# Top-32 attention and a feed-forward block on one core: VectorE turns both heads of 72 units at the end of a step, GpSimd gets the smaller scores as a difference to the larger, and TensorE's filling follows an estimate of VectorE's step

## The chip, the cores and the metric

The kernel runs on one core of one Trainium2 chip. A core has five engines that run side by side, each with its own in-order queue: TensorE (PE; its weight loads are shown as PEld), VectorE (DVE), ScalarE (ACT), GpSimd (POOL), and SyncE (SP), which here only issues DMAs. The metric is the device time of one execution in microseconds, lower is better. A profile is of one execution; "span" is the time from its first to its last instruction.

## The reference

Attention over 8 batches, 8 heads, 576 positions and a head size of 64, in which each row keeps its 32 largest scores; then a normalised feed-forward block of width 512 and 2048. All is float32.

```python
scores = scale * np.matmul(q, k.transpose(0, 1, 3, 2))
kth = np.partition(scores, -top_k, axis=-1)[..., -top_k:-top_k + 1]     # top_k = 32
scores = np.where(scores >= kth, scores, -1e9)
attn = np.exp(scores - np.max(scores, axis=-1, keepdims=True))
attn = attn / (np.sum(attn, axis=-1, keepdims=True) + 1e-09)
x = heads side by side of np.matmul(attn, v)                            # (8, 576, 512)
xn = (x - mean) / np.sqrt(var + 1e-06) * g_ln
out = x + np.maximum(xn @ w_ch1, 0.0) @ w_ch2
```

## The kernel before

**Units and steps.** Two heads are handled together. Their 576 query rows make four units of 128 rows (numbers 0 to 3) and one of 64 rows, the rest unit, which packs both heads into 128 partitions. There are 160 units. They come in groups that are multiplied with the values together: from the third batch on, the first half of a batch has four groups of units 0, 1 and rest, the second half four groups of units 2 and 3. The main loop makes one step per unit, and all engines' work is written out by hand in the order of that loop.

**A unit's way.** Unit n has its scores made by TensorE at step n-1 (`scores`: eight matmul records at line 354 into PSUM, four ScalarE copies at line 335 into the tile `sc`). Also at step n-1 `halve` splits its 576 scores into 288 pairs: VectorE takes the larger of each pair (line 376, tile `hi`), GpSimd the smaller (tile `lo`) with integer arithmetic on the bits, as a + b (line 375) minus the larger (line 377). At step n VectorE looks for the 32 largest: `select` with argument 0 works on `lo` (lines 390 and 385), with 1, 2 and 3 on `hi` (lines 398 and 385). At step n+1 ScalarE makes the mask (`mask`, line 442, tile `e`), at step n+2 the exponential with its row sum (`weigh`, line 452). At step n+2 the weights are also turned, so that keys lie on partitions (tile `pt`), and at the third step after a group's last unit `values` multiplies them with the values (lines 563 and 570).

**Turning.** `turn` gives a list of parts: four TensorE transposes for each head (line 505) with a ScalarE copy out of PSUM (line 517 for head 0, 521 for head 1), and a last one for the columns left over (lines 538 and 539). From batch 2 on, 72 units (`u.moved`: whole units that are not the last of their group) have head 1 turned otherwise, by `move`: VectorE transposes 32x32 blocks (line 482, written into the unit's own `sc`, which is free by then), SP stores the result in DRAM (line 487) and reads it back in another order into `pt` with four DMAs (line 489). `move` stands after `select(u, 0)`, early in the step, and `weigh` takes head 1 first for these units.

**Filling.** The feed-forward work on finished rows is a list of small pieces, `todo`: "hidden" matmuls at line 680 and "project" matmuls at line 697. `fill` is called eight times a step and issues pieces up to a share, `slot(n)`. Until all weights are converted (the first 18 steps) the share is the difference of the two estimates `dve_cost` and `pe_cost`; after that it is an equal amount for each step up to the next delivery of rows (`gives`), with `RESERVE` us of work kept back.

**Other names.** `prepare` makes the exponential's bias (lines 436 and 437), on VectorE for the first 17 units, on GpSimd for the others. `turn_heads` (line 304) transposes K and Q of the next pair of heads on VectorE; behind it SP loads the pair after that, eight DMAs. `stats` (lines 629 to 638) normalises finished rows, `recips` are reciprocals of row sums (line 932). Tiles of one name share a few buffers: `sc` has four, `hi` two, `lo`, `pt` one.

Of the kernel before, what the change touches and what calls it, by code (L numbers as in the profile page):

```python
# [29 lines left out]
def kernel(  # L30
# [332 lines left out]
    def halve(u):  # L363

        nt = len(u.tiles)  # L370
        u.lo = lopool.tile([P, 2, HALF], FP32, tag="lo", name="lo")
        u.hi = hipool.tile([P, 2, HALF + TOP_K // 2], FP32, tag="hi", name="hi")
        a, b = u.sc[:, 0:nt, 0:HALF], u.sc[:, 0:nt, HALF:S]
        lo, hi = u.lo[:, 0:nt], u.hi[:, 0:nt, 0:HALF]
        nc.gpsimd.tensor_tensor(lo.bitcast(I32), a.bitcast(I32), b.bitcast(I32), ALU.add)  # L375
        nc.vector.tensor_tensor(hi, a, b, ALU.max)  # L376
        nc.gpsimd.tensor_tensor(  # L377
            lo.bitcast(I32), lo.bitcast(I32), hi.bitcast(I32), ALU.subtract
        )

    def select_halved(u, i):
        nt = range(len(u.tiles))
# [46 lines left out]
    def prepare(u):  # L429

        nt = len(u.tiles)
        u.bias = small.tile([P, 2], FP32, tag="bias", name="bias")
        b = u.bias[:, 0:nt]

        engine = nc.vector if u.i < CONVERTING else nc.gpsimd
        engine.tensor_tensor(b, u.thr[:, 0:nt, 7], u.top[:, 0:nt, 0], ALU.subtract)  # L436
        engine.tensor_scalar(b, b, scale, 0.0, ALU.mult, ALU.add)  # L437

    def mask(u, t):
        if u.e is None:  # L440
# [25 lines left out]
    def place_of(u):  # L466

        g = u.group  # L470
        if g.pt is None:
            g.pt = ptpool.tile([P, 2 * J + 1, GQ], FP32, tag="pt", name="pt")
            g.ptB = g.pt[:, J : 2 * J].rearrange("p c n -> p (c n)").rearrange(
                "p (i c n) -> p i c n", c=J, n=32
            )
        return sum(P for x in g.qts if x < u.qt)

    def move(u):

        i0 = place_of(u) // 32  # L480
        t = u.sc[:, 1, 0:JP]
        nc.vector.transpose(
            t.rearrange("p (j c n) -> p j c n", j=P // 32, c=J),
            u.e[:, 1, R:S].rearrange("p (c j k) -> p j c k", c=J, k=32),
        )
        hbm = hbmpool.tile([P, JP], FP32, tag="turned", name="turned")
        nc.sync.dma_start(hbm[:], t)
        for j in range(P // 32):
            nc.sync.dma_start(
                u.group.ptB[j * 32 : (j + 1) * 32, i0 : i0 + P // 32].rearrange(  # L490
                    "k i c n -> k i (c n)"
                ),
                hbm[:, j * P : (j + 1) * P].rearrange("(i k) x -> k i x", k=32),
            )

    def turn(u):

        g = u.group
        q0 = place_of(u)
        i0 = q0 // 32  # L500

        def part(t):
            ps = turned()
            for c in range(J):
                nc.tensor.transpose(  # L505
                    ps[:, c * P : (c + 1) * P], u.e[:, t, c * P + t * R : (c + 1) * P + t * R],
                    ident[:],
                )
            if u.rest:
                both = ps[:].rearrange("p (c h n) -> p h c n", h=2, n=R)  # L510
                nc.scalar.copy(g.pt[:, 0:J, q0 : q0 + R], both[:, 0])
                nc.scalar.copy(
                    g.ptB[:, i0 : i0 + R // 32],
                    both[:, 1].rearrange("p c (i n) -> p i c n", n=32),
                )
            elif t == 0:
                nc.scalar.copy(  # L517
                    g.pt[:, 0:J, q0 : q0 + P], ps[:].rearrange("p (c n) -> p c n", n=P)
                )
            else:  # L520
                nc.scalar.copy(
                    g.ptB[:, i0 : i0 + P // 32],
                    ps[:].rearrange("p (c i n) -> p i c n", c=J, n=32),
                )

        def last():
            ps = turned()
            if u.rest:
                nc.tensor.transpose(ps[0:R, 0:P], u.e[:, 0, JP:S], ident[:])
                nc.tensor.transpose(ps[:, P : 2 * P], u.e[:, 0, JP - R : S], ident[:])  # L530
                for h in range(2):
                    nc.scalar.copy(
                        g.pt[h * R : (h + 1) * R, 2 * J, q0 : q0 + R],
                        ps[h * R : (h + 1) * R, h * (P + R) : h * (P + R) + R],
                    )
            else:
                ends = u.e[:].rearrange("p t n -> p (t n)")[:, JP : JP + P]
                nc.tensor.transpose(ps[:, 0:P], ends, ident[:])
                nc.scalar.copy(g.pt[:, 2 * J, q0 : q0 + P], ps[:, 0:P])

        heads = [0] if u.moved else range(len(u.tiles))
        return [lambda t=t: part(t) for t in heads] + [last]

    xs, xps, rs, oTr, dr = {}, {}, {}, {}, {}
# [13 lines left out]
    def values(g):  # L558
        vb = g.job.v
        av = brief("av")  # L560
        for c in range(J):
            for h in range(2):
                nc.tensor.matmul(  # L563
                    av[h * D : (h + 1) * D, 0 : g.nq],
                    vb[:, h * J + c, :],
                    g.ptB[:, 0 : g.nq // 32, c, :] if h else g.pt[:, c, 0 : g.nq],
                    start=(c == 0),
                    stop=False,
                )
        nc.tensor.matmul(  # L570
            av[:, 0 : g.nq], g.job.ends[:], g.pt[:, 2 * J, 0 : g.nq],
            start=False, stop=True,
        )
        g.oT = otpool.tile([P, GQ], FP32, tag="oT", name="oT")
        nc.scalar.copy(g.oT[:, 0 : g.nq], av[:, 0 : g.nq])
# [237 lines left out]
                add_block(step, tiles, dsts)  # L813

    SLOTS = 8
    RESERVE = 4.0
    last_give = max(gives)

    def at(i):
# [5 lines left out]
        last = at(n - 2) if n - 2 < EARLY else at(n - 3) if n - 3 >= EARLY else None  # L825
        return turned, last.group if last and last is last.group.units[-1] else None

    DVE_UNIT, DVE_REST, DVE_HALVED, DVE_MOVE = 10.3, 5.3, 0.9, 0.8


    turns = {}
# [4 lines left out]
    def pe_cost(n):  # L836
        c = 0.0
        if at(n + 1):
            c += 1.25 if at(n + 1).rest else 1.5
        ex, g = after(n)  # L840
        if ex:
            c += 0.67 if ex.rest else 0.55 if ex.moved else 1.0
        if g:
            c += 0.6 + 7.8e-3 * g.nq
        return c

    def dve_cost(n):
        u, ex = at(n), after(n)[0]
        c = 5.0 if u is None else DVE_REST if u.rest else DVE_UNIT
        if u and u.halved:  # L850
            c *= DVE_HALVED
        return c + DVE_MOVE if ex and ex.moved else c

    def give(n):
        early = not all(map(done, ready))
# [8 lines left out]
    def slot(n):  # L864


        if n <= CONVERTING:
            return max(0.0, dve_cost(n) - pe_cost(n)) / SLOTS
        left = sum(t[1] for t in todo)
        if n > last_give:  # L870
            even = left / max(1, END - 1 - n)
        else:
            even = 99.0
            for m in sorted(gives):
                if m > n:
                    even = min(even, (left - RESERVE) / (m - n))
                    left += sum(b.cost() for b in gives[m])
        return max(0.0, even) / SLOTS

    recips, rows_of = {}, {}  # L880

# [18 lines left out]
    for n in range(END):  # L900
# [12 lines left out]
        quick = ex.group if last and ex.group.quick else None  # L913

        moved = ex is not None and ex.moved
        order = (1, 0) if moved else (0, 1)
        sent, stores[:] = stores[:], []

        if ex and not early:
            weigh(ex, order[0])  # L920
        if nxt:
            scores(nxt)
        if g:
            values(g)
        if u:
            select(u, 0)
        if moved:
            move(ex)
        for store in sent:
            store()  # L930
        for den in recips.pop(n, []):
            nc.vector.reciprocal(den, den)
        if n == gives_first:
            for blk, i in rows_of.pop(n):
                blk.stats(i)
# [7 lines left out]
            weights(n, 0)  # L943
        fill()
        if ex and len(ex.tiles) > 1 and not early:
            weigh(ex, order[1])
        fill()
        if parts and not moved:
            parts[0]()
# [3 lines left out]
            select(u, 1)  # L953
        if nxt and nxt.halved:
            halve(nxt)
        if n in turns:
            turn_heads(turns[n])
            later = fresh.index(turns[n]) + 1
            if later < len(fresh):
                load(fresh[later], nc.sync, nc.sync)  # L960
        for blk, i in rows_of.pop(n, []):
            blk.stats(i)
        if not quick:
            weights(n, 1)
        fill()
        if mk and not early:
            mask(mk, int(mk.moved))
        if g:
            place(g)
        if late:  # L970
            place_rest(late.job.b, late.job.hp)
        fill(1 if g or late else 0)
        fill()
        if moved:
            parts[0]()
        elif len(parts) > 2:
            parts[1]()
        if u:
            select(u, 2)
        for blk in gives.get(n - 2, []):  # L980
            blk.inverse()
        if last and ex.group.sums is not None:
# [7 lines left out]
        if parts:  # L990
            parts[-1]()
        if mk and len(mk.tiles) > 1 and not early:
            mask(mk, 1 - int(mk.moved))
        fill()
        for x in (u if n < EARLY else None, mk if n > EARLY else None):
            if x and x is units[x.job.last]:
# [9 lines left out]
        if u:  # L1006
            select(u, 3)
            if u.i < CONVERTING:
                prepare(u)
        for x in (g, quick):  # L1010
            if x and x.job.hp == NHP - 1:
                for qt in x.qts:
# [43 lines left out]
```

## Time and profile before

The three runs took 1665.36, 1665.81 and 1666.85 us. The profiled execution has a span of 1666.8 us.

| stretch (us) | what runs | TensorE busy | VectorE busy | ScalarE busy | GpSimd busy |
|---|---|---|---|---|---|
| 0 to 130 | loads, first units, weights converted | 64.4 | 111.8 | 87.5 | 76.2 |
| 130 to 400 | all units turned by TensorE | 252.4 | 262.1 | 203.4 | 146.6 |
| 400 to 1500 | from 428.6 on with `move` | 1096.0 | 1053.1 | 735.9 | 419.1 |
| 1500 to 1667 | last units, then feed-forward alone | 161.3 | 37.6 | 50.4 | 22.1 |

Busy time counts an instruction from its start to its end on its engine. TensorE's matmuls overlap each other and their ends are modelled, so its busy time says that it had no gap, not that it ran at its best. A group line of the profile reads: source line, engine and operation; output tile <- input tile with partitions x elements; count; total busy us and mean ns of one; and how long the engine sat idle just before these instructions, with what ended the idle time.

### The profile page before, as it was taken

What the parts mean: (1) busy time and instruction counts of PE and PEld (TensorE: products, weight loads), DVE (VectorE), ACT (ScalarE), POOL (GpSimd) and SP (SyncE); (2) the same over time, 40 slices, a digit from 0 to 9 for tenths busy, and PEclk for the clock granted to TensorE, in tenths of its full rate; (3) what the DMA queues carried; (4) which work ended last, traced back from release to release, by engine and by line L of the source; (5) the groups of instructions that cost most, each with busy time, mean ns of one, the idle gap of its engine ahead of it and who ended that gap; (6) DMA issues with size and microseconds to landing.
All of it is one profiled execution on the core that took longest, in us unless ns stands there. A gap on an engine that the chain in (4) does not pass through costs nothing.

```text
span 1666.8 us, 25284 instructions
## 1 busy us (share of the span) xinstructions
PE 1574.1 (94%) x7113; PEld 955.1 (57%) x7113; DVE 1464.5 (88%) x4476; ACT 1077.2 (65%) x2759; POOL 664.0 (40%) x879
## 2 busy tenths in 40 slices
PE   3568989989999999999999999999999999999998
PEld 1346556566555575755547575745547575755564
DVE  5998999999999999999999999899998999998000
ACT  5677967767666776767666675767666676665310
POOL 5567854343433434343343434343243433333010
PEclk9758999999999999999999999999999999999999
DMA  7423333001331133213231233112331132111000
GB/s 176 100 64 108 89 58 59 22 14 27 76 81 51 53 76 81 65 54 69 59 86 51 55 73 83 52 54 70 65 89 44 53 81 74 52 46 47 26 13 13
DMA packets 301203, 104.58 MB, mean 63 GB/s; under 512 B 246276, under 2 KB 283144, under 8 KB 301064
## 3 DMA queue, kind: packets, MB, share of 16 engines
q1 hardware_dynamic: 296328, 102.39, 24.4%
q10 hardware_dynamic: 4736, 0.59, 0.3%
q8 instruction: 57, 0.93, 0.2%
q14 instruction: 82, 0.67, 0.1%
HBM read 74.58 MB, written 28.31 MB: 62 GB/s over the span
## 4 chain that ended last, share of the span: by engine, by line
PE 71%; DVE 21%; issue 4%; ACT 2%; POOL 1%; DMA 1%; ACTq 0%; POOLq 0%; DVEq 0%; SPq 0%
PE hps L680 25%; PE ops L697 24%; PE scps L354 8%; PE av L563 6%; DVE m L398 5%; DVE hi L385 4%; PE tp L505 4%; DVE hi L390 2%; DVE m L416 2%; PE av L570 2%; DVE w L423 2%; DVE lo L385 1%; DVE hi L376 1%; DVE size L188 1%; PE tp L667 1%
## 5 line engine op out<-in xcount | busy, mean ns | idle before, releaser
L680 PE MATMUL hps<-xT,w 128*128 128x256 f32 (+1 forms) x2048 | 550.0, 411 | 2.7 <-ACT xT L672 2.3
L697 PE MATMUL ops<-w,h 128*128 128x512 f32 x1152 | 546.1, 599 | 0.0
L398 DVE MAX8 m<-hi 128x8 f32<-128x304 f32 x1088 | 460.7, 458 | 2.3
L680 PEld LDWEIGHTS hps<-xT,w 128*128 128x128 f32 x2048 | 372.1, 191 | 108.5 <-issue 17.3
L385 DVE MATCH_REPLACE8 hi<-m,hi 128x304 f32<-128x304 f32 x816 | 368.0, 456 | 0.0
L375 POOL TENSOR_TENSOR lo<-sc 128x576 int32<-128x576 int32 (+1 forms) x152 | 197.7, 1301 | 316.3 <-ACT sc L335 156.9
L697 PEld LDWEIGHTS ops<-w,h 128*128 128x128 f32 x1152 | 200.2, 191 | 169.9 <-issue 164.6
L377 POOL TENSOR_TENSOR lo<-lo,hi 128x576 int32<-128x576 int32 (+1 forms) x152 | 196.8, 1295 | 141.9 <-DVE hi L376 139.7
L354 PE MATMUL scps<-kT,qT 64*128 64x288 f32 (+3 forms) x1344 | 217.4, 433 | 32.4 <-DVE qT L304 20.9
L335 ACT COPY sc<-scps 128x288 f32<-128x288 f32 x576 | 199.2, 409 | 62.3 <-PE scps L354 51.0
L442 ACT ACTIVATE e<-sc,m 128x576 f32<-128x576 f32 x288 | 224.3, 779 | 9.7 <-DVE m L398 6.2
L452 ACT ACTIVATE e<-e,bias 128x576 f32<-128x576 f32 x288 | 224.6, 780 | 2.9 <-DVE bias L437 2.5
L390 DVE MAX8 hi<-lo 128x8 f32<-128x288 f32 x544 | 221.8, 443 | 2.6 <-POOL lo L377 1.5
L354 PEld LDWEIGHTS scps<-kT,qT 64*128 64x128 f32 (+1 forms) x1344 | 122.4, 181 | 146.6 <-issue 56.2
L505 PEld LDWEIGHTS tp<-ident,e 128*128 128x128 f32 x864 | 110.9, 147 | 115.9 <-ACT e L452 51.7
L505 PE MATMUL tp<-ident,e 128*128 128x128 f32 x864 | 138.1, 285 | 38.2 <-ACT e L452 37.9
L692 ACT ACTIVATE h<-hps 128x256 f32<-128x256 f32 (+1 forms) x256 | 105.9, 414 | 96.5 <-PE hps L680 93.8
L436 POOL TENSOR_TENSOR bias<-m,m 128x2 f32<-128x2 f32 (+1 forms) x143 | 27.8, 195 | 303.6 <-DVE m L398 303.6
L563 PE MATMUL av<-pt,vb 128*64 128x256 f32 (+2 forms) x1088 | 146.7, 413 | 0.0
L376 DVE TENSOR_TENSOR hi<-sc 128x576 f32<-128x576 f32 (+1 forms) x152 | 138.8, 913 | 5.5 <-ACT sc L335 5.5
L385 DVE MATCH_REPLACE8 lo<-hi,lo 128x288 f32<-128x288 f32 x272 | 118.2, 440 | 0.0
L517 ACT COPY pt<-tp 128x512 f32<-128x512 f32 x128 | 74.6, 583 | 62.1 <-PE tp L505 60.5
(79 smaller groups left out, 1295.0 us busy)
## 6 DMA issues: line engine op xcount, KB each, us to landing
turned<-sc SPq DMA_DIRECT2D x72, 256.0 KB, 2.0
pt<-turned SPq DMA_DIRECT2D x288, 64.0 KB, 2.0
vb<-in_v_dram SPq DMA_DIRECT2D x136, 128.0 KB, 2.5
raw<-in_moe_w_ch_dram SPq DMA_DIRECT2D x32, 512.0 KB, 4.0
kin<-in_k_dram SPq DMA_DIRECT2D x128, 72.0 KB, 2.5
qin<-in_q_dram SPq DMA_DIRECT2D x120, 72.0 KB, 2.5
out_dram<-o SPq DMA_DIRECT2D x32, 256.0 KB, 2.2
ends<-in_v_dram SPq DMA_DIRECT2D x136, 16.0 KB, 2.2
```

Source lines behind the costliest of these rows:

```text
L335: nc.scalar.copy(u.sc[:, t, s * HALF : (s + 1) * HALF], made[s][t][:, 0:HALF])
L354: nc.tensor.matmul(ps[i * R : i * R + ql, o : o + width], qT[r, q0 : q0 + ql], kT[r, k0 : k0 + width], start=True, stop=True,)
L375: nc.gpsimd.tensor_tensor(lo.bitcast(I32), a.bitcast(I32), b.bitcast(I32), ALU.add)
L385: nc.vector.match_replace(x[:, t], m[:, t, :], x[:, t], LOWEST)
L390: nc.vector.max(u.hi[:, t, o : o + 8], u.lo[:, t])
L398: nc.vector.max(m[:, t, :], u.hi[:, t])
L442: nc.scalar.activation(u.e[:, t], u.sc[:, t], AF.Prelu, bias=u.thr[:, t, 7:8], scale=-1.0, alpha=SLOPE)
L452: nc.scalar.activation(u.e[:, t], u.e[:, t], AF.Exp, bias=u.bias[:, t : t + 1], scale=-scale / SLOPE, accum_out=g.den[:, col : col + 1],)
L505: nc.tensor.transpose(ps[:, c * P : (c + 1) * P], u.e[:, t, c * P + t * R : (c + 1) * P + t * R], ident[:],)
L563: nc.tensor.matmul(av[h * D : (h + 1) * D, 0 : g.nq], vb[:, h * J + c, :], g.ptB[:, 0 : g.nq // 32, c, :] if h else g.pt[:, c, 0 : g.nq], ...
L680: nc.tensor.matmul(ps["h"][:, 0:N], w1[:, c, f * P : (f + 1) * P], xT[0][:, c, 0:N], start=(c == 0), stop=(c == NC - 1),)
L697: nc.tensor.matmul(ps[i][:], hT[f][:, i * P : (i + 1) * P], w2[:, f, :], start=(f == 0), stop=(f == NF - 1),)
```

## The change

- `halve`: VectorE's maximum comes first. GpSimd then makes a minus the larger, and adds b. Both GpSimd operations now come behind the maximum; before, the first needed only the scores.
- `prepare` for the first 17 units: one fused VectorE instruction per head in place of two instructions for both.
- `move`: both heads of the 72 units are turned by VectorE (two transposes, one store of 512 KB, eight reads), at the end of the step, after `select(u, 3)`. TensorE's four transposes and ScalarE's copy (line 517) for head 0 go; `pt` holds both heads in the same layout of blocks. `weigh` and `mask` take head 0 first for all units.
- Reciprocals move behind `halve`, `stats` behind `select(u, 2)`.
- `slot`: after the first 18 steps the share makes `pe_cost` plus filling a constant multiple of an estimate of VectorE's step, smoothed over three steps (`pace`). The estimates' constants change, `RESERVE` goes from 4 to 7.

```diff
-        nc.gpsimd.tensor_tensor(lo.bitcast(I32), a.bitcast(I32), b.bitcast(I32), ALU.add)
         nc.vector.tensor_tensor(hi, a, b, ALU.max)
         nc.gpsimd.tensor_tensor(
-            lo.bitcast(I32), lo.bitcast(I32), hi.bitcast(I32), ALU.subtract
+            lo.bitcast(I32), a.bitcast(I32), hi.bitcast(I32), ALU.subtract
         )
+        nc.gpsimd.tensor_tensor(lo.bitcast(I32), lo.bitcast(I32), b.bitcast(I32), ALU.add)
...
-        engine = nc.vector if u.i < CONVERTING else nc.gpsimd
-        engine.tensor_tensor(b, u.thr[:, 0:nt, 7], u.top[:, 0:nt, 0], ALU.subtract)
-        engine.tensor_scalar(b, b, scale, 0.0, ALU.mult, ALU.add)
+        if u.i < CONVERTING:
+            for t in range(nt):
+                nc.vector.tensor_scalar(
+                    b[:, t : t + 1], u.thr[:, t, 7:8], u.top[:, t, 0:1], scale,
+                    ALU.subtract, ALU.mult,
+                )
+            return
+        nc.gpsimd.tensor_tensor(b, u.thr[:, 0:nt, 7], u.top[:, 0:nt, 0], ALU.subtract)
+        nc.gpsimd.tensor_scalar(b, b, scale, 0.0, ALU.mult, ALU.add)
...
     def move(u):
-        i0 = place_of(u) // 32
-        t = u.sc[:, 1, 0:JP]
-        nc.vector.transpose(...)
-        hbm = hbmpool.tile([P, JP], FP32, tag="turned", name="turned")
-        nc.sync.dma_start(hbm[:], t)
-        for j in range(P // 32):
-            nc.sync.dma_start(u.group.ptB[j * 32 : (j + 1) * 32, ...], hbm[:, j * P : (j + 1) * P]...)
+        i0 = place_of(u)
+        ni = P // 32
+        for t in range(2):
+            nc.vector.transpose(
+                u.sc[:, t, 0:JP].rearrange("p (j c n) -> p j c n", j=ni, c=J),
+                u.e[:, t, t * R : t * R + JP].rearrange("p (c j k) -> p j c k", c=J, k=32),
+            )
+        hbm = hbmpool.tile([P, 2, JP], FP32, tag="turned", name="turned")
+        nc.sync.dma_start(hbm[:], u.sc[:, :, 0:JP])
+        for j in range(ni):
+            for t in range(2):
+                nc.sync.dma_start(u.group.blocks[j * 32 : (j + 1) * 32, t, i0 : i0 + ni]..., hbm[:, t, ...]...)
...
-        heads = [0] if u.moved else range(len(u.tiles))
+        heads = () if u.moved else range(len(u.tiles))
...
-    DVE_UNIT, DVE_REST, DVE_HALVED, DVE_MOVE = 10.3, 5.3, 0.9, 0.8
+    DVE_UNIT, DVE_REST, DVE_HALVED, DVE_MOVE, DVE_TURN = 9.7, 5.0, 0.89, 1.4, 1.45
...
+    def pace(n):
+        return (dve_cost(n - 1) + 2 * dve_cost(n) + dve_cost(n + 1)) / 4
...
-            for m in sorted(gives):
-                if m > n:
-                    even = min(even, (left - RESERVE) / (m - n))
-                    left += sum(b.cost() for b in gives[m])
-        return max(0.0, even) / SLOTS
+        for k in range(n, last_give):
+            pe += pe_cost(k)
+            dve += pace(k)
+            if k + 1 in gives:
+                ratio = min(ratio, (left - RESERVE + pe) / dve)
+                left += sum(b.cost() for b in gives[k + 1])
+        return max(0.0, ratio * pace(n) - pe_cost(n)) / SLOTS
...
-        if moved:
-            move(ex)
         for store in sent:
             store()
-        for den in recips.pop(n, []):
-            nc.vector.reciprocal(den, den)
...
         if nxt and nxt.halved:
             halve(nxt)
+        for den in recips.pop(n, []):
+            nc.vector.reciprocal(den, den)
...
         if u:
             select(u, 2)
+        for blk, i in rows_of.pop(n, []):
+            blk.stats(i)
...
             select(u, 3)
             if u.i < CONVERTING:
                 prepare(u)
+        if moved:
+            move(ex)
```

## The prediction

> **What bounds the kernel now.** I read the share of busy time first, then the slices, then busy time by stretch, then VectorE's groups and waits.
>
> ```profile
> PE 1574.1 (94%) x7113; PEld 955.1 (57%) x7113; DVE 1464.5 (88%) x4476; ACT 1077.2 (65%) x2759; POOL 664.0 (40%) x879
> PE   3568989989999999999999999999999999999998
> DVE  5998999999999999999999999899998999998000
> ```
>
> Two engines are near full from the fourth slice on, and for the last three slices TensorE works alone. So there are three stages: a start that VectorE leads (to about 409), a long middle, and a TensorE tail. The stretch from the start of VectorE's step 40 (408.7) to that of step 158 (1517.4) is the middle; the second line below is the tail, from TensorE's step 157 on (columns: stretch, length, then busy time of PE, PEld, DVE, ACT, POOL, with counts, then clock, DMA share, GB/s).
>
> ```profile
> 408.70:1517.40 1108.70, 1104.13 (x5023) 661.41 (x5022) 1061.99 (x3319) 741.33 (x1927) 423.81 (x602) 1.00 0.25 65
> 1504.30:1666.80 162.50, 156.95 (x546) 90.64 (x545) 33.37 (x109) 48.14 (x116) 19.70 (x29) 1.00 0.08 24
> ```
>
> In the middle TensorE has no gap to speak of (4.6 of 1108.7 us), VectorE has 46.7. Who is behind?
>
> ```profile
> L482 DVE STREAM_TRANSPOSE sc<-e 128x512 f32<-128x512 f32 x72 | 50.3, 698 | 59.7 <-ACT e L452 59.4
> L376 DVE TENSOR_TENSOR hi<-sc 128x576 f32<-128x576 f32 x120 | 124.6, 1038 | 5.5 <-ACT sc L335 5.5
> L390 DVE MAX8 hi<-lo 128x8 f32<-128x288 f32 x544 | 221.8, 443 | 2.6 <-POOL lo L377 1.5
> 893.38 0.71 DVE L482 STREAM_TRANSPOSE sc<-e 128x512 f32<-128x512 f32 x1 [3.07 <-ACT e L452]
> ```
>
> VectorE waits almost only at the transpose in `move`, for ScalarE's exponential, 2 to 3 us at a time (fourth line, from the timeline). ScalarE is late because TensorE is: the wait comes where three equal portions of filling meet a short rest step. In a triple of steps (units 0, 1, rest, here steps 86 to 88) TensorE's score matmuls start 8.8, 8.0 and 11.0 us apart, 27.8 us; VectorE's own work is 11.0 + 8.3 + 6.2 = 25.5. In a pair (steps 98 and 99) both need 19.3. So TensorE leads by little: adding the gaps over 0.15 us up to 1517.4, VectorE lost 39.7 us and worked 1069.0.
>
> **What the skill says.** "SBUF — State Buffer", section "Who interferes with whom": VectorE with two SBUF inputs and GpSimd reading SBUF hold one shared port as an exclusive lock, and the later one blocks. The trace agrees: line 376's shortest run is 0.74 us, its mean 1.04, its longest 1.95, and the long ones lie beside line 375 on GpSimd; transposes and MAX8, with one input, take the same beside GpSimd (0.457 against 0.459 for MAX8). "VectorE: DVE Perf Modes", section "The three transpose paths": VectorE turns 32x32 blocks only, which is why DRAM has to reorder them; here 0.70 us for four blocks' worth of a head. "DMA: Bandwidth & Descriptors", section on the anatomy of one DMA: about 2 us are fixed, mostly the receipt. Here both DMAs of `move` have a median of 2.0 us to landing, whether 256 KB or 64 KB.
>
> **The change part by part**, against the profiled span of 1666.8, which is 1.0 above the median of the runs.
>
> *Maximum before GpSimd.* In the middle, the 118 runs of line 376 lie 30.2 us in sum above the unhindered 0.745 (whole) and 0.445 (rest); nothing of GpSimd's pair can stand beside them any more. Bounds: 30 gone, or 20 if other GpSimd work (output additions, 1.29 us) gets in the way. I take 30. The price: `lo` is ready later by GpSimd's first operation, 1.43 us. After the maximum GpSimd needs 2.9. In a step of unit 1 or 3 the maximum would start at 3.9 and end at 4.7, `lo` is there at 7.6, and the next step begins at 8.3 to 8.6. A rest step, without the transposes ahead, has 2.4 + 0.75 + 2.9 = 6.1 of 6.85. It fits, except behind an output addition (36 in all): some 0.1 us each, 4 us.
>
> *Second transpose.* 70 of the 72 lie in the middle; two that follow each other start about 0.62 apart (as a move adds 0.60 to a step): +43.4 us on VectorE. On TensorE 4 transposes at 0.109 start to start go: 70 x 0.436 = 30.5. ScalarE loses 72 copies of 0.58, 42 us, but is 67% busy there: nothing, hidden behind both.
>
> *Later place.* The wait of line 482 for ScalarE goes; it stays where ScalarE is a whole step behind: nothing. In its place two things follow the move. First, the `sc` buffer comes free only when the store has landed. By the program's own order of buffers, the copies of the second unit of each triple (24 of them) use a buffer whose store was issued one step end earlier: 2.0 to 2.7 for the landing, 1.2 to 1.5 for four copies, against a maximum at 3.9: 0 to 0.3 us, 4 us in sum. Elsewhere a full step lies between. Second, `pt`: the store, then eight reads at 0.43 on SP, then 2.0 for landing, 2.2 + 3.5 + 2.0 = 7.7 after the move. SP has also the eight K and Q loads (4.0 to 4.9 us behind `turn_heads`) and four of V (2.2) ahead of one move per group, which can hold the store for 0.7 to 1.9: up to 9.6. `values` needs `pt` one step (8.3 to 8.6) and the scores (0.65) later: TensorE is held at 0 to 0.6 us behind VectorE, and VectorE does not notice before it is about 1.9 behind (3.9 less 2.0 for scores and copies). Nothing, with the end kept for a rival.
>
> *Equal multiple.* By the program's order the filling per triple now follows VectorE (about 3.4, 7.8, 6.9 us where it was 6.0, 6.0, 6.0, the small share in the short step). It is the same work; it takes away the reason for VectorE's waits.
>
> *Middle, summed.* VectorE: 1069.0 - 30.2 + 43.4 = 1082.2. TensorE, from scores to scores (409.2 to 1526.2): 1117.0 - 30.5 = 1086.5. The two are within half a percent. I take the larger plus the 8 us of waits: 1094.5, a gain of 14.2.
>
> *Start.* The biases cost VectorE 17 x (0.697 + 0.191) = 15.1 us, since line 436 has two inputs. 34 fused ones with one input should take about 0.17 to 0.19, as line 437 does beside GpSimd: 6, gain 9; if they block like line 436, 34 x 0.7 = 24, loss 9. The maxima of steps 20 to 39 give 3.7. Against it stands that GpSimd is 71% busy from 130 to 260 and its first operation can't start early any more, and that VectorE already waited 4.5 us for scores at step 10. I take a gain of 7, from -3 to 13.
>
> *Tail.* From the scores of unit 158 on the program has 142.9 us of filling where it had 139.5, and 8 transposes fewer: +2.6.
>
> Sum: 1666.8 - 14.2 - 7 + 2.6 = 1648.2, less 1.0 to the median: **1647**.
>
> **Rivals.**
> *A, TensorE alone decides.* For: no gap in the middle; it can be ahead of VectorE at the start and loses less there. Then no wait is seen and the start gives 13, while VectorE's transposes cost 35 instead of 43: middle 1082, 1666.8 - 27 - 13 + 2 - 1 = 1628. Against: VectorE needs 1082 too.
> *B, GpSimd late.* `lo` misses the step start by 0.1 us in most of 118 steps, 12 us, and the start gives nothing: 1647 + 12 + 5 = 1664, no change. Against: 0.7 to 1 us of room in each step.
> *C, slower: the round trip through DRAM.* The chain move, store, eight reads, `values` decides as soon as it lasts more than some 10.5 us after the step's end (8.6 + 1.9), 0.9 above my upper end. The reads' longest issue was 2.1 us and longest landing 3.8, so it can. Then TensorE and after it VectorE stop in each of 48 groups; at 0.6 us, 29 us: 1676. Against: the medians.
> *D, it does not do what it says:* the estimates mislead the filling, and steps mismatch as before, so that 20 of the 39.7 us of waits stay: 1647 + 12 = 1659.
>
> **Chances.** The forecast (1638 to 1656) 0.48, A 0.18, D 0.12, B 0.10, C 0.12. The range 1628 to 1664 leaves C and the edges out. 0.2% is 3.3 us, about what a measurement of this kernel can tell: faster by more 0.79 (forecast, A, most of D, a little of B), within 0.09, slower 0.12.
>
> **What would show it.** Line 376 at a mean of 0.75 for whole units; the transposes of `move` at 144, with no wait above 1 us for ScalarE; TensorE's line 505 at 576 and ScalarE's copy of line 517 gone for moved units; VectorE's idle time in the middle below 20 us. Wrong if VectorE waits at line 376 for `sc`, at line 390 for `lo`, or TensorE at line 563 for a DMA, each for more than 10 us in sum.

## The result, and the profile after

The changed kernel takes 1683.83 us (1679.77 to 1685.19), the kernel before 1666.15 beside it: a ratio of 1.0102, with a 95% interval of 1.0084 to 1.0120. It is 1% slower, where 1% faster was forecast. The profiled execution has a span of 1682.4 us, 15.6 more than before; all sums below are made against the spans.

Start with the page of the changed kernel: busy time by engine, and the slices of TensorE and VectorE.

```profile
PE 1562.3 (93%) x6825; PEld 939.6 (56%) x6825; DVE 1473.0 (88%) x4547; ACT 1032.2 (61%) x2687; POOL 660.8 (39%) x879
PE   3569899999799999999999999999999999999998
DVE  6998999999799999999989999899999999996100
```

TensorE has 288 matmul records less, as it should with 72 x 4 transposes gone, and VectorE is busier by 8.5 us. Neither explains a longer span. Both engines now have a 7 in the eleventh slice (421 to 463), in the middle, where both had 9 before. The chain of waits, that is the chain that ended last, shares out the span by engine; here for the kernel before, and then after.

```profile
PE 71%; DVE 21%; issue 4%; ACT 2%; POOL 1%; DMA 1%; ACTq 0%; POOLq 0%; DVEq 0%; SPq 0%
```

```profile
DVE 61%; PE 17%; DMA 8%; issue 5%; ACT 4%; POOL 3%; SPq 1%; ACTq 0%; DVEq 0%; POOLq 0%
DVE m L398 18%; DVE hi L385 15%; DVE hi L390 8%; PE hps L684 8%; DMA turned<-sc 5%; DVE lo L385 5%; DVE sc L489 4%; DVE hi L375 4%; PE ops L701 4%; PE av L567 3%; ACT sc L335 2%; DVE m L416 1%; DMA pt<-turned 1%; PE scps L354 1%; DVE w L423 1%
```

The chain went through TensorE for most of the span; now it goes through VectorE, and 8% of it is DMA, 5% the store of the turned weights. The same shows in the groups by form (columns as in the prediction; line 375 is now the maximum, 489 the transposes of `move`, 567 the multiplication with the values).

```profile
L335 ACT COPY sc<-scps 128x288 f32<-128x288 f32 x576 | 198.5, 411 | 98.4 <-PE scps L354 55.1 <-DMA turned<-sc 32.5 <-PE hps L684 2.0
L375 DVE TENSOR_TENSOR hi<-sc 128x576 f32<-128x576 f32 x120 | 92.3, 769 | 40.3 <-ACT sc L335 40.3
L489 DVE STREAM_TRANSPOSE sc<-e 128x512 f32<-128x512 f32 x144 | 93.5, 684 | 32.1 <-ACT e L458 32.1
L567 PE MATMUL av<-pt,vb 128*64 128x320 f32 x448 | 77.7, 464 | 30.8 <-DMA pt<-turned 25.8 <-ACT sc L335 3.0 <-DMA dr<-den 1.8
L390 DVE MAX8 hi<-lo 128x8 f32<-128x288 f32 x544 | 221.2, 443 | 11.3 <-POOL lo L379 9.8
```

The maximum is cheap now (769 ns, it was 1038), but VectorE stands 40.3 us in front of it for ScalarE's copies, of which 22.7 us lie in the middle. The copies stand 32.5 us for the store (`turned<-sc`), which was no releaser of theirs before. TensorE stands 25.8 us for `pt` in this form, 27.2 in all.

The DMA issues (DMA, engine, count, KB each, median us to landing):

```profile
turned<-sc SPq DMA_DIRECT2D x72, 512.0 KB, 3.1
pt<-turned SPq DMA_DIRECT2D x576, 64.0 KB, 2.0
```

The store of 512 KB lands in 3.1 us; that of 256 KB took 2.0 before.

What this does in one place is seen in the timeline. First the hold of `sc`, in lines picked from the window 1442 to 1456 of the changed kernel (start, length, engine and line, operation; in brackets the wait ahead of it and what ended it).

```profile
1442.00 1.28 DVE L489 STREAM_TRANSPOSE sc<-e 128x512 f32<-128x512 f32 x2
1443.31 0.56 SPq L494 DMA_DIRECT2D turned<-sc  x1
...
1447.71 1.31 ACT L335 COPY sc<-scps 128x288 f32<-128x288 f32 x4 [3.11 <-DMA turned<-sc]
1447.81 3.64 SPq L497 DMA_DIRECT2D pt<-turned  x8
...
1449.05 0.76 DVE L375 TENSOR_TENSOR hi<-sc 128x576 f32<-128x576 f32 x1 [1.85 <-ACT sc L335]
```

The transposes write into the unit's `sc`, SP stores it, and the copies of a later unit's scores need that buffer. They start when the store has landed, 4.4 us after its issue here, and VectorE loses 1.85 us at its maximum. Next the way of `pt`, from the window 436 to 466.

```profile
436.55 1.29 DVE L489 STREAM_TRANSPOSE sc<-e 128x512 f32<-128x512 f32 x2
...
439.12 0.58 SPq L494 DMA_DIRECT2D turned<-sc  x1
...
442.66 3.66 SPq L497 DMA_DIRECT2D pt<-turned  x8
...
447.73 4.73 PE L567 MATMUL av<-pt,vb 128*64 128x320 f32 x16 [9.44 <-DMA pt<-turned]
...
453.77 0.42 ACT L579 COPY oT<-av 128x320 f32<-128x320 f32 x1 [9.74 <-PE av L574]
...
459.36 0.78 ACT L710 ACTIVATE o<-ops,mv,rstd 128x512 f32<-128x512 f32 x1 [4.57 <-PE ops L701]
...
460.03 0.76 ACT L458 ACTIVATE e<-e,bias 128x576 f32<-128x576 f32 x1
...
460.92 0.71 DVE L489 STREAM_TRANSPOSE sc<-e 128x512 f32<-128x512 f32 x1 [7.58 <-ACT e L458]
```

The move ends at 437.8; the store is issued 1.3 later (SP was still issuing loads of V) and lands 3.5 us after that, the eight reads take 3.7 us to issue, and `pt` is whole at 447.7, 9.9 us after the move. TensorE had stood still for 9.44 us. VectorE pays for it later in the step. ScalarE stands for TensorE's late products, first 9.74 us for `av` and then 4.57 for a filling matmul, before it gets to the exponential, and so VectorE waits 7.58 us for ScalarE at its second transpose.

The same three stages as in the prediction, cut at VectorE's step 40 and step 158:

| stretch | before | after | difference |
|---|---|---|---|
| start of the span to step 40 | 408.7 | 398.8 | -9.9 |
| the middle, step 40 to 158 | 1108.7 | 1132.4 | +23.7 |
| of it VectorE's work | 1069.0 | 1086.7 | +17.7 |
| of it VectorE's waits over 0.15 us | 39.7 | 45.7 | +6.0 |
| step 158 to the end | 149.4 | 151.1 | +1.7 |

By what ended them, VectorE's waits in the middle are now 22.7 us at the maximum for the copies, 15.2 at the transposes of `move` for ScalarE's exponential, and 7.8 at line 390 for `lo` (before: none, 38.3 and 1.5). The 15.2 us all lie in five steps, and in each of these TensorE had stood still for `pt`.

### The profile page after: what moved, and what is told of

The parts are those of the page before. It is cut to its first block, busy times and chain, and to the rows that moved or that the text cites. A ratio compares the mean times of both kernels' runs of the same rounds, so it can differ in the third digit from the quotient of the medians.

```text
span 1682.4 us, 24965 instructions
## 1 busy us (share of the span) xinstructions
PE 1562.3 (93%) x6825; PEld 939.6 (56%) x6825; DVE 1473.0 (88%) x4547; ACT 1032.2 (61%) x2687; POOL 660.8 (39%) x879
## 4 chain that ended last, share of the span: by engine, by line
DVE 61%; PE 17%; DMA 8%; issue 5%; ACT 4%; POOL 3%; SPq 1%; ACTq 0%; DVEq 0%; POOLq 0%
DVE m L398 18%; DVE hi L385 15%; DVE hi L390 8%; PE hps L684 8%; DMA turned<-sc 5%; DVE lo L385 5%; DVE sc L489 4%; DVE hi L375 4%; PE ops L701 4%; PE av L567 3%; ACT sc L335 2%; DVE m L416 1%; DMA pt<-turned 1%; PE scps L354 1%; DVE w L423 1%
## 5 line engine op out<-in xcount | busy, mean ns | idle before, releaser
L684 PE MATMUL hps<-xT,w 128*128 128x256 f32 (+1 forms) x2048 | 541.7, 409 | 3.1 <-ACT xT L676 2.0
L376 POOL TENSOR_TENSOR lo<-sc,hi 128x576 int32<-128x576 int32 (+1 forms) x152 | 196.6, 1293 | 565.7 <-DVE hi L375 302.5
L354 PE MATMUL scps<-kT,qT 64*128 64x288 f32 (+3 forms) x1344 | 224.2, 433 | 29.6 <-DVE qT L304 16.2
L379 POOL TENSOR_TENSOR lo<-lo,sc 128x576 int32<-128x576 int32 (+1 forms) x152 | 194.7, 1281 | 11.9
L567 PE MATMUL av<-pt,vb 128*64 128x256 f32 (+2 forms) x1088 | 158.7, 422 | 33.4 <-DMA pt<-turned 27.2
L375 DVE TENSOR_TENSOR hi<-sc 128x576 f32<-128x576 f32 (+1 forms) x152 | 108.9, 716 | 40.3 <-ACT sc L335 40.3
L567 PEld LDWEIGHTS av<-pt,vb 128*64 128x64 f32 x1088 | 85.4, 144 | 100.5 <-issue 49.5
L513 PE MATMUL tp<-ident,e 128*128 128x128 f32 x576 | 95.2, 292 | 34.9 <-ACT e L458 34.6
L579 ACT COPY oT<-av 128x256 f32<-128x256 f32 (+2 forms) x68 | 26.2, 386 | 161.9 <-PE av L574 161.9
L513 PEld LDWEIGHTS tp<-ident,e 128*128 128x128 f32 x576 | 74.9, 150 | 89.6 <-ACT e L458 48.0
L489 DVE STREAM_TRANSPOSE sc<-e 128x512 f32<-128x512 f32 x144 | 93.5, 684 | 32.1 <-ACT e L458 32.1
```

Source lines behind the costliest of these rows:

```text
L354: nc.tensor.matmul(ps[i * R : i * R + ql, o : o + width], qT[r, q0 : q0 + ql], kT[r, k0 : k0 + width], start=True, stop=True,)
L376: nc.gpsimd.tensor_tensor(lo.bitcast(I32), a.bitcast(I32), hi.bitcast(I32), ALU.subtract)
L379: nc.gpsimd.tensor_tensor(lo.bitcast(I32), lo.bitcast(I32), b.bitcast(I32), ALU.add)
L567: nc.tensor.matmul(av[h * D : (h + 1) * D, 0 : g.nq], vb[:, h * J + c, :], g.blocks[:, h, 0 : g.nq // 32, c, :], start=(c == 0), stop=False,)
L684: nc.tensor.matmul(ps["h"][:, 0:N], w1[:, c, f * P : (f + 1) * P], xT[0][:, c, 0:N], start=(c == 0), stop=(c == NC - 1),)
```

## Experiments

Two theories stand against each other. One: the round trip of the turned weights (store, its landing, eight reads, their landing) is too long for the late place of `move`; it holds `sc` and delays `pt`. The other: the trip is hidden, and the new filling, the second transposes or the order of the maximum cost the time. The ratios are to the kernel before beside it, with the 95% interval.

**The move earlier** (a_early). The only edit: `move` stands behind `select(u, 2)`, 2.3 us earlier in the step.

```diff
             blk.stats(i)
+        if moved:
+            move(ex)
         for blk in gives.get(n - 2, []):
...
             select(u, 3)
-        if moved:
-            move(ex)
```

> The changed kernel with move one place earlier, behind select(u, 2) instead of behind select(u, 3); the same work on every engine. Theory 1 (the late place: the 512 KB store holds the sc buffer 3.1 to 4.4 us past the step's end, and the reads of pt come late): the waits of VectorE for sc at its maximum go from 22.7 us in the middle to under 4, TensorE's wait for pt from 27 to under 4, and the time is 1648 to 1660. Theory 2 (VectorE's added transposes are what costs): 1678 or more, as VectorE's work is the same.

Measured: 1663.90 us, ratio 0.9983 (0.9974 to 0.9993), 20 us less than the changed kernel. VectorE's waits in the middle fell from 45.7 to 32.0, those at the maximum for `sc` from 22.7 to 4.5; the copies waited 16.2 us for the store instead of 32.5, and TensorE's 27.2 us for `pt` are gone. The time lies between the two ranges expected: 19.1 us of waits for ScalarE's exponential now stand at the transposes. The place is part of the cause: the same instructions, 2.3 us earlier, are worth 20 us.

**Two stores in place of one** (a_split). At the late place, each head's weights are stored as soon as they are turned, 256 KB each, and head 0 is read back first.

```diff
         for t in range(2):
             nc.vector.transpose(...)
-        hbm = hbmpool.tile([P, 2, JP], ...)
-        nc.sync.dma_start(hbm[:], u.sc[:, :, 0:JP])
-        for j in range(ni):
-            for t in range(2):
+            hbms.append(hbmpool.tile([P, JP], ...))
+            nc.sync.dma_start(hbms[t][:], u.sc[:, t, 0:JP])
+        for t in range(2):
+            for j in range(ni):
                 nc.sync.dma_start(...)
```

> The changed kernel with one store of 256 KB for each head, the first issued as soon as its transpose is done; place unchanged. Theory 1: landing falls from 3.1 to 2.0 to 2.4, so the copies to sc start about 0.7 earlier after a step's end, VectorE's waits for sc fall from 22.7 to under 8, and the time is 1664 to 1675. Theory 2: no change, 1680 to 1686.

Measured: 1655.47 us, ratio 0.9928 (0.9910 to 0.9947), 28 us less than the changed kernel with the same bytes and one DMA more per move; it is below the 1664 to 1675 expected. Its groups by form and its store:

```profile
L335 ACT COPY sc<-scps 128x288 f32<-128x288 f32 x576 | 198.7, 411 | 84.0 <-PE scps L354 55.8 <-DMA turned<-sc 10.6 <-DVE hi L390 5.6
L375 DVE TENSOR_TENSOR hi<-sc 128x576 f32<-128x576 f32 x120 | 92.1, 767 | 24.6 <-ACT sc L335 24.4
```

```profile
turned<-sc SPq DMA_DIRECT2D x144, 256.0 KB, 2.1
```

The copies' wait for the store went from 32.5 to 10.6, VectorE's at the maximum from 40.3 to 24.4 (in the middle from 22.7 to 6.8), TensorE's for `pt` from 27.2 to 11.6. Counted from the end of the move to the start of the first read's issue and to the end of the last one's, the medians are 3.32 and 7.19 us in the changed kernel, 1.64 and 5.64 here: head 0's store is on its way while head 1 is being turned, and each store lands a microsecond sooner. The new order of the reads, head 0 first, was not tried by itself.

**Both** (a_early_split): the two stores at the earlier place.

> Both edits on the changed kernel: one store per head, and move behind select(u, 2). Theory 1 (what cost was the hold on sc and on ScalarE behind it by one large store at the step's end): with the small stores little is left of it, and the earlier place adds waits of VectorE for ScalarE's second exponential (19 us with the one large store): 1650 to 1658, no better than the split alone by more than 5. If the reads of pt were the larger part: another 8 to 12 below the split, 1643 to 1648.

Measured: 1650.02 us, ratio 0.9895 (0.9878 to 0.9911). It beats both kernels, is within 0.2% of the forecast of 1647, and is 5.5 us below the split alone, a little more than the 5 expected if the hold were all. VectorE's middle is 1098.3 us, 1081.2 of work and 17.2 of waits. Its chain by engine, from the page:

```profile
PE 60%; DVE 27%; issue 4%; POOL 3%; ACT 3%; DMA 2%; SPq 1%; ACTq 0%; POOLq 0%; DVEq 0%
```

DMA's share is back from 8% to 2%, and TensorE carries most of the chain again. Nothing of the rest of the change was touched, so what the changed kernel lost was lost through the place of `move` and its round trip.

**What the rest of the change does.** The maximum ahead of GpSimd alone, in the kernel before (b_halve):

```diff
-        nc.gpsimd.tensor_tensor(lo.bitcast(I32), a.bitcast(I32), b.bitcast(I32), ALU.add)
         nc.vector.tensor_tensor(hi, a, b, ALU.max)
-        nc.gpsimd.tensor_tensor(lo..., lo..., hi..., ALU.subtract)
+        nc.gpsimd.tensor_tensor(lo..., a..., hi..., ALU.subtract)
+        nc.gpsimd.tensor_tensor(lo..., lo..., b..., ALU.add)
```

> The kernel before with the maximum ahead of GpSimd's two operations, nothing else. VectorE's maximum falls to a mean of 0.75 for whole units and its work in the middle by 30. If TensorE leads the middle (my reading of the profile before): VectorE's waits rise by about as much and only the start gains, 1658 to 1664. If VectorE led it after all: 1630 to 1640.

Measured: 1669.43 us, ratio 1.0014 (1.0005 to 1.0022). In the middle VectorE's work fell from 1069.0 to 1045.7 and its waits rose from 39.7 to 62.0; its groups by form show where, and its chain by engine which engine leads.

```profile
L375 DVE TENSOR_TENSOR hi<-sc 128x576 f32<-128x576 f32 x120 | 93.2, 777 | 6.4 <-ACT sc L335 6.0
L482 DVE STREAM_TRANSPOSE sc<-e 128x512 f32<-128x512 f32 x72 | 50.4, 700 | 72.0 <-ACT e L452 71.6
L390 DVE MAX8 hi<-lo 128x8 f32<-128x288 f32 x544 | 222.9, 446 | 15.0 <-POOL lo L379 13.9
PE 72%; DVE 18%; issue 5%; ACT 3%; POOL 2%; DMA 1%; ACTq 0%; POOLq 0%; DVEq 0%; SPq 0%
```

The 23 us that VectorE no longer loses at the maximum are waited away, one half at the transpose of `move` (in the middle from 38.3 to 48.9), the other at line 390 for `lo`, which GpSimd now finishes later (from 1.5 to 12.5). TensorE has no more of a gap in the middle than before (busy in 1103.2 of 1107.7 us) and carries 72% of the chain: it set the pace of the kernel before, as the prediction read it. The time is above the 1658 to 1664 expected; the start, up to step 40, gained only 0.9 us.

The old order in the split version (a_split_unhalve: the same three lines the other way round, in a_split).

> One store per head, with GpSimd's sum ahead of the maximum as it was. If VectorE leads the middle now, the maximum's 30 us of blocking come back in full or nearly: 1675 to 1686, and VectorE's waits for lo (10.8) go. If TensorE still leads: under 1662.

Measured: 1678.72 us, ratio 1.0070 (1.0055 to 1.0085), 23 us more than a_split. In the middle the runs of the maximum stand 24.8 us above the prediction's unhindered times (0.745 us, and 0.445 in a rest step), against 2.3 in a_split. Where VectorE sets the pace, the same edit is worth its full price.

The old share of filling, in the changed kernel (a_even) and in the split version (a_split_even): `slot` hands out equal amounts and `RESERVE` is 4.

```diff
-        for k in range(n, last_give):
-            pe += pe_cost(k)
-            dve += pace(k)
-            ...
-        return max(0.0, ratio * pace(n) - pe_cost(n)) / SLOTS
+        for m in sorted(gives):
+            if m > n:
+                even = min(even, (left - RESERVE) / (m - n))
+                left += sum(b.cost() for b in gives[m])
+        return max(0.0, even) / SLOTS
```

> The changed kernel with the old slot, equal filling per step and RESERVE 4, all else as changed. Theory 1: the multiple is right and missed by the hold; with equal shares TensorE's step no longer fits VectorE's, the lag between the two swings by 4 us each way as before the change, and VectorE waits more: 1688 to 1705. Theory 3 (the multiple underfeeds TensorE and is what made it slower): 1650 to 1675.

> One store per head, with the old slot and RESERVE 4. Theory 1: the multiple is worth 10 to 25 us where nothing else holds: 1665 to 1680. Theory 3: under 1652.

Measured: 1705.83 us, ratio 1.0226 (1.0208 to 1.0245), and 1670.42, ratio 1.0021 (1.0013 to 1.0029); the first is 1 us above its range. The equal multiple, with its `RESERVE` of 7, saves 22 us in the changed kernel and 15 in the split one. The theory that the new filling is what costs is out.

Head 0 back on TensorE (a_one): VectorE turns head 1 alone, at the late place, stores 256 KB and reads four blocks; two constants of the estimates are set for one head, all else is as changed.

```diff
-        for t in range(2):
+        for t in (1,):
             nc.vector.transpose(...)
...
-        heads = () if u.moved else range(len(u.tiles))
+        heads = (0,) if u.moved else range(len(u.tiles))
...
-            c += ... 0.15 if ex.moved ...
+            c += ... 0.55 if ex.moved ...
```

> The changed kernel with head 0 back on TensorE: one transpose by VectorE, one store of 256 KB, four reads, still at the step's end; the planner's two constants for it set back. VectorE's work in the middle falls by 43, TensorE's rises by 30. Theory 2: 1640 to 1650 (all of VectorE's share comes back). Theory 1: VectorE's waits for sc are under 5 as the store is small, TensorE leads again, 1650 to 1660.

Measured: 1670.28 us, ratio 1.0016 (1.0009 to 1.0023). VectorE's work in the middle is 1047.4, 39.3 less than in the changed kernel, and its waits are 68.2. The time lies above both ranges expected. The copies wait only 2.6 us for the store, yet VectorE waits at the maximum:

```profile
L375 DVE TENSOR_TENSOR hi<-sc 128x576 f32<-128x576 f32 x120 | 91.6, 763 | 64.2 <-ACT sc L335 63.5
```

Scores are late here because TensorE is: in the middle its score matmuls start on average 0.83 us behind VectorE's step, where they are 1.04 ahead in the changed kernel. Without the second transposes TensorE is the bound again (busy in 1108.8 of the middle's 1115.6 us), and the time is near that of the kernel before. By itself this run can't say what the transposes cost, since it halves the store and the reads as well. The split version can: it keeps them, and is 15 us faster than a_one. So the second transposes are not the loss either.

**The size of the store by itself.** The store of 512 KB in a_one (a_one_big) and in the kernel before (b_big). It carries head 0's old scores beside head 1's weights, and nobody reads that half.

```diff
-        hbm = hbmpool.tile([P, JP], ...)
-        nc.sync.dma_start(hbm[:], u.sc[:, 1, 0:JP])
+        hbm = hbmpool.tile([P, 2, JP], ...)
+        nc.sync.dma_start(hbm[:], u.sc[:, :, 0:JP])
```

> Head 0 on TensorE, one transpose by VectorE at the step's end as in the run with one head, but the store takes 512 KB (head 1's turned weights and, beside them, head 0's old scores, which nobody reads back): VectorE's and TensorE's work and the four reads are those of the run with one head, only the store is doubled. Theory 1 (the size of a store at the step's end is what holds sc and ScalarE): landing 3.0 to 3.2, ScalarE's waits for the store go from 2.6 us to over 20, and the time is 1676 to 1690 against 1670. Theory 2 (the added transposes and reads are what costs): 1668 to 1672.

> The kernel before with the store doubled to 512 KB in the same way, at the old early place in the step. Theory 1: a buffer that is not needed for most of a step can be held 1 us longer: 1665 to 1668, no change. If the traffic itself were what costs (128 KB... 256 KB more for each of 72 units): over 1670.

Measured: 1673.02 us, ratio 1.0039 (1.0024 to 1.0054), and 1667.36, ratio 1.0005 (0.9996 to 1.0014). In both the store's landing went from 2.0 to 3.1 us; this is the DMA line of b_big, at the old place and with nothing else changed.

```profile
turned<-sc SPq DMA_DIRECT2D x72, 512.0 KB, 3.1
```

A microsecond more of landing costs nothing that can be measured at the early place, and some 3 us at the late one while TensorE sets the pace (the intervals of a_one and a_one_big just miss each other). The expectation for a_one_big was missed: I had taken the hold to cost the same wherever the move is late. It doesn't; where the scores come late anyway, the store has mostly landed by then (the copies waited 6.3 us for it, not 32.5).

**Hold or lateness.** The round trip can hurt in two ways, by holding `sc` and by delivering `pt` late. The first run delays `pt` alone: a_split_reread reads head 1's blocks once ahead of head 0's and once more after, twelve reads in place of eight, with the stores as in a_split.

```diff
-        for t in range(2):
+        for t in (1, 0, 1):
             for j in range(ni):
                 nc.sync.dma_start(...)
```

> One store per head as before, but head 1's reads go first, then head 0's, and head 1's four reads are issued once more at the end (the same bytes to the same place): sc comes free as early as with the split, while pt is complete later than in the changed kernel itself (12 issues of 0.43 us behind the second landing, against 8 behind one landing of 3.1: some 0.9 us later). If the hold on sc is the cause: 1652 to 1664, near the split alone. If the lateness of pt is: 1682 or more. In between: both, in that share.

Measured: 1714.76 us, ratio 1.0294 (1.0258 to 1.0331), 59 us more than a_split. The last read is issued 8.89 us after the move instead of 5.64. From its waits (who <- for whom: us, count, longest):

```profile
DVE sc L490 <- ACT e L458: 64.4, 21, 11.3
PE av L568 <- DMA pt<-turned: 50.1, 35, 10.7
```

Of the 64.4 us, 47.5 lie in the middle, where a_split has 5.3; the rest is in the tail of both. The copies waited 8.7 us for the stores, no more than in a_split, and TensorE 50.1 for `pt` (11.6). Late `pt` is enough to lose the time; until then I had taken the hold of `sc` for the main cause. This run also puts 50% more reads on SP and the DMA engines, and how much of the 59 us is theirs isn't separated.

It suggested that the lateness of `pt` alone decides: 5.64, 7.19 and 8.89 us stand against 1655, 1684 and 1715, a straight line of 18 us for each microsecond. The last run holds `sc` and leaves `pt` nearly where it was: a_split_hold stores head 1 a second time, to a place that nobody reads, behind the first read.

```diff
                 nc.sync.dma_start(...)
+                if (t, j) == (0, 0):
+                    again = hbmpool.tile([P, JP], ...)
+                    nc.sync.dma_start(again[:], u.sc[:, 1, 0:JP])
```

> The split version, in which SP stores head 1's turned weights a second time, to a place in DRAM that nobody reads, right after the first of the eight reads. So `sc` comes free only when that third store has landed, about 1.64 + 0.43 + 0.35 + 2.0 = 4.4 us after the move (2.9 in the split version, about 3.5 in the changed kernel), while the last read is issued only some 0.35 us later (5.64 -> 6.0; 7.19 in the changed kernel). If only the lateness of `pt` costs time, at about 18 us for each us of it: 1655 + 6 = 1661. If the hold of `sc` costs as well, VectorE's waits at the maximum for `sc` rise from 6.8 us to more than the changed kernel's 22.7 and the time to 1672 or more.

Measured: 1696.82 us, ratio 1.0181 (1.0164 to 1.0198), 41 us more than a_split, with the last read issued at 5.87 us, only 0.23 later. Its waits:

```profile
ACT sc L335 <- DMA again<-sc: 67.5, 23, 5.5
DVE hi L375 <- ACT sc L335: 59.7, 29, 12.5
...
PE av L571 <- DMA pt<-turned: 18.0, 16, 6.4
```

So the straight line does not hold by itself (it would have given 1660; the last read has also landed only 0.3 to 0.4 us later than in a_split), and the hold is a cause of its own. That the third store's 256 KB of traffic costs the time by itself is not ruled out by a run at this place; at the early place, in b_big, as much more cost nothing. The third store is issued 2.0 us after the move and lands in 2.3. With a landing from the medians, `sc` is free 2.1 us after the move in a_split, 3.1 in the changed kernel, 4.3 here, and VectorE's waits at the maximum in the middle are 6.8, 22.7 and 42.3 us.

Each way, made longer by itself, costs more than the changed kernel lost. The changed kernel has both, a microsecond more of hold and one and a half more of lateness than a_split, worth 28 us together. At the rate of these runs (41 us for 2.2 us of hold, 59 for 3.25 of lateness, 18 to 19 for a microsecond of either) the two would add up to 47, so they don't simply add. By what ended VectorE's waits in the middle, those at the maximum fell by 15.9 us from the changed kernel to a_split and those at the transposes by 9.9. But one kind brings the other with it: late `pt` alone, in a_split_reread, also raised the waits at the maximum to 17.1. How the 28 us divide stays open. Turning into a tile of its own, which would leave `sc` unheld, was not tried.

## Why the prediction was wrong

**What bounds the kernel before: right.** b_halve took 23 us of work from VectorE and got nothing for them.

**Maximum before GpSimd: right.** Forecast -30.2 us on VectorE; the excess fell from 30.2 to 2.1. The price, `lo` later, was put at 4 us, a little behind each output addition. It was 7.8 us in three waits at line 390, and the one of 2.75 us at 464 follows from TensorE's stop at 447, which had made the output addition ahead of it late.

**Second transpose: right.** Forecast work of VectorE in the middle 1082.2; measured 1086.7. Of the 4.5 us between them 2.1 are what is left of the maximum's excess, which the sum took away whole; the rest was not traced.

**Equal multiple: right** that it takes away waits; a_even and a_split_even put 22 and 15 us on it and its `RESERVE`.

**Start: right, and a little low.** Forecast a gain of 7 (-3 to 13), measured 9.9; the fused biases take 0.204 us each beside GpSimd, above the 0.17 to 0.19 and far from the 0.7 of a blocked one. b_halve alone gains 0.9 by step 40, so the maxima give less than the 3.7 put down for them. **Tail: right**, +2.6 forecast, +1.7 measured.

**Later place: wrong, and nearly all of the miss lies here.** The sum had 1094.5 us for the middle. With 1082.2 of work that leaves 12.3 for waits: 4 for the hold, 4 for `lo`, and 4.3 by which TensorE was to lead. There were 45.7: 22.7 at the maximum for `sc`, 15.2 at the transposes in the five steps with a late `pt`, and 7.8 for `lo`. This 33.4 more and the 4.5 of work are the 37.9 us by which the middle came out too long. Two terms of this step were mis-sized, and both rest on the round trip:

- *The hold of `sc`*, priced at "2.0 to 2.7 for the landing" and 4 us in sum. The landing took 3.1 (a median), and the store's issue was up to 1 us late in nine of ten moves. With 1.3 for the copies that is 4.4 to 5.4 against a maximum at 3.9: 0.5 to 1.5 us, not 0 to 0.3. The number of places, 24, was nearly right: of 27 waits 16 stand at the second unit of a triple, 6 at that of the first pair behind the triples, and 5 elsewhere.
- *The way of `pt`*, put at 2.2 + 3.5 + 2.0 = 7.7, up to 9.6, and priced at "Nothing, with the end kept for a rival". The sum counts the last read's 0.43 twice, as landing runs from the start of the issue: it stands for 7.3. The first read was issued at 3.32 after the move, not 2.2, and the last had landed at 8.8 as a median and 10.1 in one move of ten.

Rival C, the round trip that decides, had the right chain of waits, with its condition and its number off. It put the limit at 10.5 us after the step's end and a stop of 0.6 us in each of 48 groups. Only 3 of 72 moves took longer than 10.5; TensorE stood for `pt` 11 times, up to 9.44 us, and VectorE in five steps. C left the hold at the forecast's 4 us, where the waits at the maximum for `sc` came to 22.7, so that its 1676 comes near the measured time is in part luck. "Against: the medians" was said of the medians of a 256 KB store. Of the three signs of being wrong that the prediction named, two showed: VectorE at the maximum for `sc`, and TensorE at the multiplication with the values for a DMA. (Rival B's sum gives back 5 us for the start where 7 had been put down; it would be 1666.)

The size of the store was on the table. The prediction took the landing of `move`'s DMAs "whether 256 KB or 64 KB" for 2.0 and gave the doubled store 2.0 to 2.7. The Trainium skill, "DMA: Bandwidth & Descriptors", section "Anatomy of one DMA — SWDGE (gpsimd) path", fits 2.0 us plus the bytes over 436 GB/s, for DMAs issued by GpSimd (these are issued by SP): an estimate of 2.6 us for 256 KB and 3.2 for 512. The traces measure 2.0 to 2.1 and 3.1, so the page is high for the small store and right for the large one; its growth with the bytes was what the step left out.

The step also priced the two links as if a miss cost its own length once. It does not stop there: TensorE and VectorE have the same amount of work in the middle (1086.5 and 1082.2 forecast) and alternate in the lead, so a stop of either can be given on to the other, as TensorE's stop of 9.44 us at 447 became one of 7.58 of VectorE at 460. With the trip shortened, the same sums hold: a_early_split spends 1081.2 of work and 1098.3 in the middle (forecast 1082.2 and 1094.5), and 1650.0 in all (1647).

## What to carry to other kernels

When two engines are brought to the same amount of work, every buffer and every round trip between them has to be priced again at the new place, with the landing of the new size and the DMA queue's own delays, from the 90th percentile and not from the median: slack that was the slower engine's is gone. A tile that serves as the source of a store is held until the store has landed, so a store put behind the last use should be cut and issued piece by piece as the data comes. And a saving on an engine is worth its full price only where that engine leads: the same three lines were worth nothing in one kernel and 23 us in another.

## What was unexpected of the hardware

One store of 512 KB from 128 partitions lands in 3.1 us and each of two stores of 256 KB in 2.1, although the second is issued 0.6 us behind the first: cut in two, the whole is there 2.2 us after the second transpose instead of 3.1. Issuing costs SP too: a 512 KB store takes 0.57 us of its queue and a 256 KB store 0.34 in the profile, each of the 64 KB reads about 0.43.
